# Integer seed of a root in one step, a moved offset, and two first-layer blocks whose high parts come first

## Chip, cores and metric

One Trainium2 chip; the program runs on one core. The metric is the device time of one execution in microseconds (us), taken as the median of several runs; lower is better. Times inside the program are microseconds from the start of the profiled span.

## What is computed

The input `u` has 2048 rows of 512 channels. Two blocks with residuals follow each other:

```
h  = u + S4D(layernorm(u))            # long convolution along the 2048 rows, + D_skip * input
x  = layernorm(h)                     # input of the mixer
t  = gelu(layernorm(x) @ w1)          # 512 -> 512
x1 = x + shift(t) @ w2                # channel quarters shifted by +1, -1, +2, -2 rows
out = h + x1 + gelu(layernorm(x1) @ w3) @ w4     # 512 -> 1792 -> 512
```

Each layernorm needs, for each row, 1/sqrt(variance + 1e-5). Everything is in 32 bits.

## The kernel before

**Two phases.** The convolution phase (`conv_phase`) takes the first 302 us or so. There a planner (`Plan`) with costs and due times sets the order of the instructions. Its last two nodes are `finish(3)` (mean and variance of rows 12 to 15 of each partition, called tiles 12 to 15) and `norm_h` (their roots); they are planned with costs of 0.4 and 2.35. The mixer phase (`mixer_phase`) has its order written out by hand: each engine gets its instructions in the order of the Python calls (class `InOrder`).

**The mixer's first part.** The 2048 rows are 16 tiles of 128 rows in four groups of four; they are worked in the order of groups 3, 0, 1, 2. For a group `q`:

- `finish(q)` computes the statistics and `norms(nc, cst, [q])` the roots, on VectorE (DVE). `norms` writes `ra` (two rows of variances), then `rsqrt_ops` turns them into `rr` with `rb` as scratch, and a last operation makes the offset `rn` = -mean * `rr`. All are tiny: 128 partitions by 8 values. `norms` is called four times, once for each group. `norm2_ops` calls `rsqrt_ops` for the second layernorm, also once for each group, with tiles `qa`, `qb`, `qr`.
- `norm1(q)` normalises the four tiles into `xq`. In group 3, tiles 12, 13 and 15 are normalised on DVE from the mean and `rr` alone; tile 14 is normalised on ScalarE (ACT), which needs the offset `rn`.
- For groups 3 and 0, `turn1(q)` transposes the tiles on TensorE (PE). For groups 1 and 2, `swap` transposes 32x32 blocks on DVE and then moves them with 16 DMAs from the SP and POOL queues. Either way four column chunks come out. Each is split into a high part (rounded, on ACT) and a low part (the rest, on DVE): for group 1 these are `xt10h` to `xt13h` and `xt10l` to `xt13l`.
- `layer1(q, f)` computes output block `f` of the first matrix: 12 matmuls into one PSUM bank. For each of four chunks these are high weight by high input, high weight by low input, low weight by high input. Then `gelu` reads the bank on ACT twice and on DVE once. In the trace, the bank is `l`; the weights live in old buffers of the convolution (`cs0w`, `cs1w`, `sn0w`). In two blocks, (3, 0) and (1, 3), the 12 matmuls are sorted: for (1, 3) all eight with a high input come first, then the four with a low input. The next block, (1, 1), takes them chunk by chunk.
- `layer2(j)` is the shifted second matrix for tile `j`.

After that come 14 steps of the last two matrices, by a scheme with sums of half matrices (`layer3a`, `layer3b`, `layer4a`, `layer4b`); PE banks there are `l3a` to `l3g`, `acc` and `l`.

PSUM banks named `bank` rotate through four buffers, so a block's bank is free once the block four before it has been read.

Of the kernel before, what the change touches and what calls it, by code (L numbers as in the profile page):

```python
# [13 lines left out]
I32 = mybir.dt.int32  # L14
AF = mybir.ActivationFunctionType
ALU = mybir.AluOpType
# [83 lines left out]
class Plan:  # L100
# [15 lines left out]
    def add(self, eng, cost, fn, r=(), w=(), at=None, bank=0, frees=None, dense=1.0, port=None, issue=0):  # L116
        n = len(self.nodes)
        deps = set()
        for k in r:
            if k in self.writer:  # L120
                deps.add(self.writer[k])
            self.readers.setdefault(k, []).append(n)
        for k in w:
            if k in self.writer:
                deps.add(self.writer[k])
            deps.update(self.readers.pop(k, ()))
            self.writer[k] = n
        deps.discard(n)
        if frees is not None:
            deps.add(frees)  # L130
        self.nodes.append(dict(eng=eng, cost=cost, fn=fn, deps=deps, at=at, bank=bank, frees=frees, dense=dense, issue=issue,
                               port=eng == "POOL" if port is None else port))
        return n
# [131 lines left out]
def rsqrt_ops(nc, v, eps, r, a, b):  # L265

    ops = [] if v is None else [lambda: nc.vector.tensor_scalar(a, v, eps, None, ALU.add)]  # L270
    ops += [
        lambda: nc.vector.tensor_scalar(b.bitcast(I32), a.bitcast(I32), 1, None, ALU.logical_shift_right),
        lambda: nc.vector.tensor_scalar(
            r.bitcast(I32), b.bitcast(I32), -1.0, float(0x5E824D95), ALU.mult, ALU.add),
        lambda: nc.vector.tensor_tensor(b, r, r, ALU.mult),
        lambda: nc.vector.scalar_tensor_tensor(b, b, 64.0 / 9.0, a, ALU.mult, ALU.mult),
        lambda: nc.vector.scalar_tensor_tensor(b, b, -10.0 / 3.0, b, ALU.add, ALU.mult),
        lambda: nc.vector.scalar_tensor_tensor(r, b, 5.0, r, ALU.add, ALU.mult),
        lambda: nc.vector.tensor_tensor(b, r, r, ALU.mult),
        lambda: nc.vector.scalar_tensor_tensor(b, b, -0.5, a, ALU.mult, ALU.mult),  # L280
        lambda: nc.vector.scalar_tensor_tensor(r, b, 1.5, r, ALU.add, ALU.mult),
    ]
    return ops
# [9 lines left out]
def norms(nc, cst, qs):  # L293

    ra, rb, rr, nb = cst["norm"]
    mv, t = cst["mv"], slice(qs[0] * 4, qs[-1] * 4 + 4)
    return [
        lambda: nc.vector.tensor_scalar(ra[:, 0, t], mv[:, t, 1], EPS, None, ALU.add),
        lambda: nc.vector.tensor_scalar(ra[:, 1, t], mv[:, t, 1], 1.0 + EPS, EPS * EPS, ALU.mult, ALU.add),
        *rsqrt_ops(nc, None, None, rr[:, :, t], ra[:, :, t], rb[:, :, t]),  # L300
        lambda: nc.vector.scalar_tensor_tensor(
            nb[:, :, t], mv[:, t, 0].unsqueeze(1).to_broadcast([128, 2, len(qs) * 4]), -1.0, rr[:, :, t], ALU.mult, ALU.mult),
    ]
# [3 lines left out]
def conv_phase(ctx, tc, cst, tp, h, x, log_A_real, A_imag, C_real, C_imag, log_dt, D_skip, w1, w2, fa, fi, tb, mm_):  # L307
# [4 lines left out]
    nc = InOrder(tc)  # L312
# [8 lines left out]
    add = plan.add  # L321
# [11 lines left out]
    NG, NS = D // CH, len(WID)  # L333
    OFF = [sum(WID[:s]) for s in range(NS + 1)]
    TS = [NOM["t0"]]
# [5 lines left out]
    at = tile("at", [128, 2, 32 * W])  # L341
# [609 lines left out]
    bx, mv = bs[:, :, 0, :], cst["mv"]  # L951
# [129 lines left out]
    for s in range(NS):  # L1081
# [18 lines left out]
        else:  # L1100

            for i, j in enumerate(range(12, 16)):
                add("DVE", 0.48, lambda j=j: v.bn_stats(bs[:, j, 0, :], h[:, j, 0 : OFF[s]]),
                    r=[("h", q, r) for q in range(s) for r in range(WID[q] // 32)] + [("made", s, BS[i])], w=[("bs", j)],
                    at=TS[s] + NOM["st"] + 2 * j)
            last_a_inv(s)

    def finish(q, tiles=range(4)):

        for j in (4 * q + i for i in tiles):  # L1110
            if q < 3:
                v.bn_stats(bs[:, j, 0, :], h[:, j, :])
        for j in (4 * q + i for i in tiles):
            v.bn_aggr(cst["mv"][:, j, :], bs[:, j, 0, :] if q < 3 else bs[:, j].rearrange("p a b -> p (a b)"))

    def norm_h():
        for op in norms(nc, cst, [3]):
            op()


    add("DVE", 0.4, lambda: finish(3), r=["part"], w=["mv"], at=TS[NS])
    add("DVE", 2.35, norm_h, r=["mv"], w=["norm"], at=TS[NS])
    plan.filler = busy
    plan.run()
    return finish
# [3 lines left out]
def mixer_phase(ctx, tc, cst, h, out, finish, w3, w4):  # L1129

    nc = InOrder(tc)
# [13 lines left out]
    def slot(i):  # L1145
        return cst["slab"](i)
# [10 lines left out]
    def bank(name):  # L1157
        return ps.tile([128, 512], F32, tag="bank", name=name)
# [18 lines left out]
    PROD = ((0, 0), (0, 1), (1, 0))  # L1177
    W1, W2 = cst["w1"], cst["w2"]


    mv = cst["mv"]
    _, _, rr, nb = cst["norm"]
# [28 lines left out]
    H1, XL, XT = {}, {}, {}  # L1211

    def norm1(q):
        XL[q] = []
        for j in range(q * 4, q * 4 + 4):
            t = quarter(XQ[{3: 0, 0: 1, 1: 2, 2: 0}[q]], j % 4)
            if (q < 2 and j % 2) or (q == 3 and j != 14):
                nc.vector.tensor_scalar(t, h[:, j, :], mv[:, j, 0:1], r12[:, j : j + 1], ALU.subtract, ALU.mult)
            else:
                nc.scalar.activation(t, h[:, j, :], AF.Identity, scale=r12[:, j : j + 1], bias=off12[:, j : j + 1])  # L1220
            XL[q].append(t)
# [21 lines left out]
        return hi, lo  # L1243

    def layer1(q, f, later=False):
        b = bank(f"l1_{q}_{f}")
        n = 0
        seq = [(c, wi, xi) for c in range(4) for wi, xi in PROD]
        if (q, f) in ((3, 0), (1, 3)):

            seq.sort(key=lambda k: 2 * k[0] + (3 if q == 3 else 8) * k[2])
        for c, wi, xi in seq:
            nc.tensor.matmul(b, W1[f][wi][:, c * 128 : c * 128 + 128], XT[q][c][xi], start=(n == 0), stop=(n == 11))
            n += 1
        *H1[q, f], low = gelu(b, f"h1_{q}_{f}")
        if later:
            return low
        low()

        tiles = {0: ((15, 0),), 2: ((14, 1), (15, 2)), 1: ((0, 3),), 3: ((0, 4), (1, 5))}[f]  # L1260
        for t, i in tiles:
            if t // 4 != q:
                continue
            for k in range(2):
                src = H1[q, f][k][:, t % 4 * 128 : t % 4 * 128 + 128]
                dst = wrap[k][i // 4][:, i % 4, :]
                if f in (0, 2):
                    nc.gpsimd.tensor_copy(dst[:, 32:128], src[:, 0:96].bitcast(F32))
                    nc.gpsimd.tensor_copy(dst[:, 1:32], src[:, 96:127].bitcast(F32))
                    nc.gpsimd.tensor_copy(dst[:, 0:1], zero)  # L1270
                else:
                    nc.gpsimd.tensor_copy(dst[:, 0:96], src[:, 32:128].bitcast(F32))
                    nc.gpsimd.tensor_copy(dst[:, 96:127], src[:, 1:32].bitcast(F32))
                    nc.gpsimd.tensor_copy(dst[:, 127:128], zero)
# [97 lines left out]
    def raw3(s):  # L1372
        f = s % half
        for i in range(2):
            o = (f + i * half) * 128
            nc.sync.dma_start(raw["ab"[i]].rearrange("p (c f) -> p c f", c=4),
                              w3[:, o : o + 128].rearrange("(c p) f -> p c f", p=128))
# [9 lines left out]
    def load3(s, low=nc.gpsimd, parts=range(3)):  # L1387
        ra, a22, sm_ = raw["a"], raw["b"][:, 256:512], raw["s"]
        if s % 2:
            one, four, last = (slot(11), slot(14)), (slots(4, 2), slots(6, 2)), slot(8)  # L1390
        else:
            one, four, last = (slot(20), W3S[0]), (slots(16, 2), slots(18, 2)), W3S[1]
        for i, (src, (hi, lo)) in enumerate(((ra, one), (sm_, four), (a22, (last[:, 0:256], last[:, 256:512])))):
            if i not in parts:
                continue
            nc.scalar.copy(hi, src)
            low.tensor_tensor(lo, src, hi.bitcast(F32), ALU.subtract)
        at_ = lambda w, i: w[:, i * 256 : i * 256 + 256]
        W3[s] = dict(a11=[at_(w, 0) for w in one], a12=[at_(w, 1) for w in one], a22=[at_(last, i) for i in range(2)],
                     **{f"s{i + 1}": [at_(w, i) for w in four] for i in range(4)})  # L1400
# [14 lines left out]
    def slots(i, n):  # L1415

        k = min(i // 3, 5)
        slot(i)
        o = (i - 3 * k) * 512 + (96 if k == 5 else 0)
        return cst["buffers"][k][:, o : o + n * 512]  # L1420
# [10 lines left out]
    low()  # L1431
    layer2(0), layer2(1)
    norm1(2), sum3()
    third = swap(XQ[0], XQ[1], queues=(nc.sync, nc.gpsimd))
    layer1(1, 3), layer1(1, 1), layer1(1, 0), layer1(1, 2), load3(0), raw3(1)
    layer2(2), layer2(3)
    XT[2] = [parts(v, f"xt2{c}") for c, v in enumerate(third)]
    norm2(0), layer2(4), layer2(5)
# [13 lines left out]
    part = lambda n: [lambda c=c: halve(FT[0, "sums", c][n], 0, n, c) for c in range(2)]  # L1452
# [191 lines left out]
```

## Time and profile before

| | |
|---|---|
| median of 3 runs (lowest, highest) | 690.0 us (689.76, 690.05) |
| profiled execution | 689.87 us |
| its span, first to last instruction | 688.1 us |
| outside the span | 1.77 us |
| mean granted TensorE clock | 0.993 |
| PE busy | 651.2 us (95%) |
| DVE busy | 548.6 us (80%) |
| ACT busy | 408.2 us (59%) |
| POOL busy | 405.0 us (59%) |

The busy share is an average over both phases. What a change in the mixer's first part is worth has to be read there: from the rows in order of time, from what ends each wait of PE, and from the chain of work that ended last. A row of the timeline has its start, its length, the engine, the operation with output and inputs, a count, and in brackets the idle time of the engine before it with what ended it. PEld is the weight load of a matmul, which runs ahead of it; a wait of PE shows there. A row that ends with "x2" merges two instructions.

### The profile page before, as it was taken

The page shows a single profiled execution, that of the slowest core. Times are in us where ns is not written, and L with a number is a line of the kernel's source. Part 1 is how long each engine was busy: PE and PEld are TensorE (multiplying, and loading weights), DVE is VectorE, ACT ScalarE, POOL GpSimd, SP SyncE. Part 2 cuts the span into 40 slices and gives each one's busy share as a digit, 9 for nine tenths or more (in the row PEclk, how much of TensorE's full clock was granted, in tenths as well). Part 3 has the DMA queues.
Part 4 walks back from the last instruction along what each step waited for, and adds up shares of the span by engine and source line. Part 5 has one row for each costly group of instructions (what it writes and reads, how often), then busy time and mean ns, then how long its engine had stood idle before and what let it go on. Part 6 is the DMA issues. An engine that isn't in the chain of part 4 may idle for free.

```text
span 688.1 us, 16792 instructions
## 1 busy us (share of the span) xinstructions
PE 651.2 (95%) x6806; PEld 507.6 (74%) x6806; DVE 548.6 (80%) x960; ACT 408.2 (59%) x706; POOL 405.0 (59%) x422
## 2 busy tenths in 40 slices
PE   5897989999999997989999999999999999999997
PEld 5894756663677684748788888888888888888885
DVE  5998999999898998989978799766879954454554
ACT  7889878967889876245634455544465543444330
POOL 1889589967999999002586209355635555554210
PEclk9998999999999999999999999999999999999999
DMA  8830554011201134010231411133311342211004
GB/s 214 255 149 2 172 169 110 3 48 32 64 3 49 34 96 108 1 60 4 62 92 47 107 31 37 56 93 103 100 44 40 106 130 62 62 46 47 19 13 122
DMA packets 49265, 51.49 MB, mean 75 GB/s; under 512 B 6436, under 2 KB 33060, under 8 KB 49188
## 3 DMA queue, kind: packets, MB, share of 16 engines
q1 hardware_dynamic: 47524, 47.80, 24.2%
q10 hardware_dynamic: 1152, 1.57, 0.9%
q0 software_dynamic: 512, 1.05, 0.6%
q8 instruction: 53, 0.87, 0.5%
q14 instruction: 24, 0.20, 0.1%
HBM read 35.72 MB, written 8.39 MB: 64 GB/s over the span
## 4 chain that ended last, share of the span: by engine, by line
PE 58%; DVE 19%; ACT 12%; issue 4%; POOL 3%; DMA 2%; SPq 1%; DVEq 0%; ACTq 0%; POOLq 0%
PE l L87 19%; PE acc L87 11%; PE bank L87 8%; ACT pt L87 7%; DVE u L87 4%; PE l3e L87 3%; PE l3b L87 3%; PE l3c L87 3%; PE l3a L87 3%; PE l3g L87 3%; PE l3f L87 3%; PE l3d L87 3%; DVE at L87 3%; DVE cs L87 3%; DMA h<-in_A_u_dram 2%
## 5 line engine op out<-in xcount | busy, mean ns | idle before, releaser
L87 ACT ACTIVATE pt<-pt 128x1056 f32<-128x1056 int32 x64 | 69.8, 1091 | 14.4 <-DVE cs L87 6.5
L87 POOL TENSOR_TENSOR pt<-p,s 128x512 int32<-128x512 int32 x64 | 71.8, 1139 | 5.0 <-DVE sn L87 4.1
L87 PE MATMUL bank<-at,tbs 128*64 128x128 f32 (+1 forms) x768 | 63.1, 311 | 3.3 <-DVE u L87 1.6
L87 PEld LDWEIGHTS bank<-at,tbs 128*64 128x64 f32 x768 | 44.6, 134 | 20.5 <-ACT at L87 2.9
L87 PEld LDWEIGHTS bank<-ident 128*128 128x128 f32 x418 | 51.5, 202 | 8.4 <-issue 5.1
L87 PE MATMUL bank<-ident 128*128 128x128 f32 x418 | 55.5, 290 | 0.0
L87 PE MATMUL bank<-u,ms 64*128 64x128 f32 x768 | 50.5, 280 | 3.5 <-DVE at L87 1.3
L87 PEld LDWEIGHTS bank<-u,ms 64*128 64x128 f32 x768 | 45.3, 187 | 8.2 <-issue 1.8
L87 POOL TENSOR_TENSOR cs0w<-raw,cs0w 128x512 fp32r<-128x512 f32 x7 | 9.1, 1300 | 58.9 <-ACT cs0w L87 47.4
L87 DVE TENSOR_TENSOR cs<-pt,amx 128x512 f32<-128x512 f32 x64 | 40.9, 679 | 2.4 <-ACT pt L87 1.3
L87 POOL TENSOR_TENSOR sn1w<-raw,sn1w 128x512 fp32r<-128x512 f32 x7 | 9.6, 1365 | 53.3 <-ACT sn1w L87 40.0
L87 DVE TENSOR_TENSOR h<-h,l 128x512 f32<-128x512 f32 x48 | 32.0, 685 | 10.6 <-PE l L87 10.6
L87 PEld LDWEIGHTS bank<-cs 128*32 128x32 f32 x1024 | 23.9, 111 | 22.0 <-POOL cs L87 6.1
L87 PE MATMUL bank<-cs 128*32 128x64 f32 x1024 | 32.5, 225 | 8.0 <-DVE cs L87 4.6
L87 DVE TENSOR_TENSOR u<-u,l3f 128x512 f32<-128x512 f32 x14 | 9.5, 682 | 36.8 <-PE l3f L87 36.8
L87 ACT ACTIVATE pt<-pt,halfpi 128x1056 f32<-128x1056 f32 x32 | 38.2, 1192 | 0.5
L87 ACT COPY at<-bank 128x512 f32<-128x512 f32 x40 | 24.9, 630 | 22.2 <-PE bank L87 22.1
L87 POOL TENSOR_TENSOR sn<-pt,amp 128x512 f32<-128x512 f32 x30 | 36.8, 1227 | 1.4 <-ACT pt L87 1.0
L87 DVE STREAM_TRANSPOSE at<-bank 128x512 f32<-128x512 f32 (+1 forms) x40 | 35.6, 919 | 2.0 <-PE bank L87 2.0
L87 ACT ACTIVATE u<-u 128x512 f32<-128x512 f32 x56 | 35.4, 632 | 1.8
L87 PE MATMUL bank<-sn 128*32 128x64 f32 x1024 | 31.8, 222 | 2.5 <-DVE sn L87 2.5
L87 POOL TENSOR_TENSOR cs<-pt,amp 128x512 f32<-128x512 f32 x26 | 31.9, 1229 | 3.5 <-ACT at L87 0.9
(1161 smaller groups left out, 2085.3 us busy)
## 6 DMA issues: line engine op xcount, KB each, us to landing
raw<-in_B_w_dram SPq DMA_DIRECT2D x28, 256.0 KB, 2.9
xq<-xq SPq DMA_DIRECT2D x72, 64.0 KB, 2.0
h<-in_A_u_dram SPq DMA_DIRECT2D x32, 128.0 KB, 4.2
h<-in_A_u_dram SPq DMA_DIRECT2D x16, 256.0 KB, 4.0
rawa<-in_B_w_dram SPq DMA_DIRECT2D x14, 256.0 KB, 2.8
rawb<-in_B_w_dram SPq DMA_DIRECT2D x14, 256.0 KB, 2.8
ms<-in_mm_dram SPq DMA_DIRECT2D x4, 768.0 KB, 11.0
out_dram<-h SPq DMA_DIRECT2D x48, 64.0 KB, 1.7
```

What stands on the lines that cost most here:

```text
L87: ins = f(*args, **kw)
```

## The change

1. `rsqrt_ops` made its integer seed in two steps: shift right by one, then multiply by -1 and add a constant. Now it is one step: multiply the integer by -0.5 and add the constant. There is one DVE instruction less in each of eight roots (four of `norms`, four of `norm2_ops`).
2. For group 3, `norm_h` leaves out the offset (the last operation of `norms`); `norm1(3)` issues it right after the first normalised tile, 12. The planned cost of `norm_h` goes from 2.35 to 1.95.
3. Blocks (1, 3) and (1, 1) are issued together (`layer1_two`): the eight matmuls with a high input of the first, the eight of the second, the four with a low input of the first, the four of the second, and then both activations. The second block now goes by highs first as well.

```
 rsqrt_ops:
-        lambda: nc.vector.tensor_scalar(b.bitcast(I32), a.bitcast(I32), 1, None, ALU.logical_shift_right),
         lambda: nc.vector.tensor_scalar(
-            r.bitcast(I32), b.bitcast(I32), -1.0, float(0x5E824D95), ALU.mult, ALU.add),
+            r.bitcast(I32), a.bitcast(I32), -0.5, float(0x5E824D95), ALU.mult, ALU.add),
...
 norm_h:
-        for op in norms(nc, cst, [3]):
+        for op in norms(nc, cst, [3])[:-1]:
             op()
...
-    add("DVE", 2.35, norm_h, r=["mv"], w=["norm"], at=TS[NS])
+    add("DVE", 1.95, norm_h, r=["mv"], w=["norm"], at=TS[NS])
...
 norm1:
                 nc.vector.tensor_scalar(t, h[:, j, :], mv[:, j, 0:1], r12[:, j : j + 1], ALU.subtract, ALU.mult)
+                if j == 12:
+                    norms(nc, cst, [3])[-1]()
...
+    def layer1_two(q, fs):
+
+        seq = [(c, wi, xi) for x in range(2) for c in range(4) for wi, xi in PROD if xi == x]
+        banks = [bank(f"l1_{q}_{f}") for f in fs]
+        for part in (seq[:8], seq[8:]):
+            for f, b in zip(fs, banks):
+                for c, wi, xi in part:
+                    nc.tensor.matmul(b, W1[f][wi][:, c * 128 : c * 128 + 128], XT[q][c][xi],
+                                     start=(c, wi, xi) == seq[0], stop=(c, wi, xi) == seq[-1])
+        for f, b in zip(fs, banks):
+            activate(q, f, b)
...
-    layer1(1, 3), layer1(1, 1), layer1(1, 0), layer1(1, 2), load3(0), raw3(1)
+    layer1_two(1, (3, 1)), layer1(1, 0), layer1(1, 2), load3(0), raw3(1)
```

`activate` is the second half of `layer1`, made a function of its own.

**DVE, end of the convolution and begin of the mixer.** `mvh` holds mean and variance of each tile, `ra`, `rb`, `rr`, `rn` are those of `norms`, `xq` are the normalised tiles. Before:

```order
L87 BN_AGGR mvh<-bs 128x2 x4
L87 TENSOR_SCALAR ra<-mvh 128x4 x2
L87 TENSOR_SCALAR rb<-ra 128x2x4
L87 TENSOR_SCALAR rr<-rb 128x2x4
L87 TENSOR_TENSOR rb<-rr 128x2x4
L87 SCALAR_TENSOR_TENSOR rb<-rb,ra 128x2x4
L87 SCALAR_TENSOR_TENSOR rb<-rb 128x2x4
L87 SCALAR_TENSOR_TENSOR rr<-rb,rr 128x2x4
L87 TENSOR_TENSOR rb<-rr 128x2x4
L87 SCALAR_TENSOR_TENSOR rb<-rb,ra 128x2x4
L87 SCALAR_TENSOR_TENSOR rr<-rb,rr 128x2x4
L87 SCALAR_TENSOR_TENSOR rn<-mvh,rr 128x2x4
```

The three tiles on DVE follow, in one piece. Now the same place reads, from `ra` on:

```order
L87 TENSOR_SCALAR ra<-mvh 128x4 x2
L87 TENSOR_SCALAR rr<-ra 128x2x4
L87 TENSOR_TENSOR rb<-rr 128x2x4
L87 SCALAR_TENSOR_TENSOR rb<-rb,ra 128x2x4
L87 SCALAR_TENSOR_TENSOR rb<-rb 128x2x4
L87 SCALAR_TENSOR_TENSOR rr<-rb,rr 128x2x4
L87 TENSOR_TENSOR rb<-rr 128x2x4
L87 SCALAR_TENSOR_TENSOR rb<-rb,ra 128x2x4
L87 SCALAR_TENSOR_TENSOR rr<-rb,rr 128x2x4
L87 TENSOR_SCALAR xq_3946<-h,mvh,rr 128x512
L87 SCALAR_TENSOR_TENSOR rn<-mvh,rr 128x2x4
L87 TENSOR_SCALAR xq_3946<-h,mvh,rr 128x512 x2
```

The first `rb` is gone, and `rn` stands behind tile 12, ahead of tiles 13 and 15. Everything that DVE does ahead of this place keeps its order, and so does everything on PE, ACT, POOL and SP up to here.

**PE, first two blocks of group 1.** `l_1_3` and `l_1_1` are the banks of blocks (1, 3) and (1, 1); the first input is the chunk, `h` or `l` at its end for high or low. Before:

```order
L87 MATMUL l_1_3_4401<-xt10h,sn0w 128x512 x2
L87 MATMUL l_1_3_4401<-xt11h,sn0w 128x512 x2
L87 MATMUL l_1_3_4401<-xt12h,sn0w 128x512 x2
L87 MATMUL l_1_3_4401<-xt13h,sn0w 128x512 x2
L87 MATMUL l_1_3_4401<-xt10l,sn0w 128x512
L87 MATMUL l_1_3_4401<-xt11l,sn0w 128x512
L87 MATMUL l_1_3_4401<-xt12l,sn0w 128x512
L87 MATMUL l_1_3_4401<-xt13l,sn0w 128x512
L87 MATMUL l_1_1_4420<-xt10h,cs0w 128x512
L87 MATMUL l_1_1_4420<-xt10l,cs0w 128x512
```

Now, from the last chunk of the first block's highs on:

```order
L87 MATMUL l_1_3_4397<-xt13h,sn0w 128x512 x2
L87 MATMUL l_1_1_4398<-xt10h,cs0w 128x512
L87 MATMUL l_1_1_4398<-xt10h,cs1w 128x512
L87 MATMUL l_1_1_4398<-xt11h,cs0w 128x512
L87 MATMUL l_1_1_4398<-xt11h,cs1w 128x512
L87 MATMUL l_1_1_4398<-xt12h,cs0w 128x512
L87 MATMUL l_1_1_4398<-xt12h,cs1w 128x512
L87 MATMUL l_1_1_4398<-xt13h,cs0w 128x512
L87 MATMUL l_1_1_4398<-xt13h,cs1w 128x512
L87 MATMUL l_1_3_4397<-xt10l,sn0w 128x512
L87 MATMUL l_1_3_4397<-xt11l,sn0w 128x512
L87 MATMUL l_1_3_4397<-xt12l,sn0w 128x512
```

The first low input is now the 17th of 24 matmuls and no longer the ninth. The instructions behind these two blocks keep their order on PE, ACT, POOL and SP.

**DVE, second layernorm of group 0.** `mv` holds the statistics of its four tiles, `qa`, `qb`, `qr` are the root's tiles. It is the fifth of the eight roots; before:

```order
L87 TENSOR_SCALAR qa<-mv_0_4351 128x4
L87 TENSOR_SCALAR qb<-qa 128x4
L87 TENSOR_SCALAR qr<-qb 128x4
L87 TENSOR_TENSOR qb<-qr 128x4
L87 SCALAR_TENSOR_TENSOR qb<-qb,qa 128x4
L87 SCALAR_TENSOR_TENSOR qb<-qb 128x4
```

Now:

```order
L87 TENSOR_SCALAR qa<-mv_0_4347 128x4
L87 TENSOR_SCALAR qr<-qa 128x4
L87 TENSOR_TENSOR qb<-qr 128x4
L87 SCALAR_TENSOR_TENSOR qb<-qb,qa 128x4
L87 SCALAR_TENSOR_TENSOR qb<-qb 128x4
```

One operation fewer stands ahead of the ACT operations that use this root; on DVE nothing but such rows and the moved `rn` differs between the two programs.

More of the change, by code (lines that the diff above doesn't have):

```diff
@@ L1245, in layer1, with activate @@
     def layer1(q, f, later=False):
+        seq = [(c, wi, xi) for c in range(4) for wi, xi in PROD]
+        if (q, f) == (3, 0):
+            seq.sort(key=lambda k: 2 * k[0] + 3 * k[2])
         b = bank(f"l1_{q}_{f}")
[L1247 to L1252, printed above, removed]
-            nc.tensor.matmul(b, W1[f][wi][:, c * 128 : c * 128 + 128], XT[q][c][xi], start=(n == 0), stop=(n == 11))
-            n += 1
+        for n, (c, wi, xi) in enumerate(seq):
+            nc.tensor.matmul(b, W1[f][wi][:, c * 128 : c * 128 + 128], XT[q][c][xi], start=(n == 0), stop=(n == 11))
+        return activate(q, f, b, later)
+    def layer1_two(q, fs):
[8 more added lines that the diff above has]
+            activate(q, f, b)
+    def activate(q, f, b, later=False):
         *H1[q, f], low = gelu(b, f"h1_{q}_{f}")
```

## The prediction

> **What bounds the kernel now.** I read the page first, then the chain that ended last in order of time, then the waits of PE's weight loads.
>
> ```profile
> span 688.1 us, 16792 instructions
> PE 651.2 (95%) x6806; PEld 507.6 (74%) x6806; DVE 548.6 (80%) x960; ACT 408.2 (59%) x706; POOL 405.0 (59%) x422
> ```
>
> PE is busy for 95% of the span; that average says nothing on a single stage. The chain does (start, length, what):
>
> ```profile
> 302.75 0.18 DVE rb L87
> ...
> 302.96 0.19 DVE rr L87
> ...
> 304.38 0.18 DVE rr L87
> ...
> 304.58 0.06 DVE rn L87
> ...
> 304.69 0.05 DVEq L87
> ...
> 304.79 0.05 DVEq L87
> ...
> 304.89 1.46 DVE xq L87 x3
> ...
> 339.22 0.61 DVE xt13l L87
> ...
> 339.88 57.68 PE l L87 x253
> ```
>
> From here to 339.83 it runs mostly on DVE (DVEq is its queue's wait instructions); from 339.88 it stays on PE to the end but for the last store. The weight loads show where PE waits between:
>
> ```profile
> 310.19 0.19 PEld L87 LDWEIGHTS l<-xt33l,cs0w 128*128 128x128 f32 x1 [0.24 <-DVE xt33l L87]
> ...
> 336.60 0.41 PEld L87 LDWEIGHTS l<-xt10h,sn0w 128*128 128x128 f32 x2
> ...
> 338.12 0.30 PEld L87 LDWEIGHTS l<-xt13h,sn0w 128*128 128x128 f32 x2 [0.17 <-ACT xt13h L87]
> ...
> 339.87 0.19 PEld L87 LDWEIGHTS l<-xt13l,sn0w 128*128 128x128 f32 x1 [0.42 <-DVE xt13l L87]
> ...
> 413.36 0.19 PEld L87 LDWEIGHTS acc<-cs0w,h_010l 128*128 128x128 f32 x1 [0.33 <-DVE h_010l L87]
> ...
> 525.56 0.19 PEld L87 LDWEIGHTS l<-sn1w,h_501h 128*128 128x128 f32 x1 [0.18 <-DVE u L87]
> ```
>
> At 310.19 PE takes the last low part of group 3. Then it doesn't wait again until group 1 arrives, with its highs at ACT's pace and its lows at DVE's. Behind 340 it waits twice more, for 0.33 and 0.18 us. So all that is gained ahead of 340 reaches the end, if nothing is late behind it.
>
> **Step 1, group 3's root and offset.** The rows above give the root's pace: `rb` to `rr` is 302.96 - 302.75 = 0.21 us, which the shorter seed saves. Tile 12 starts 0.51 behind the last `rr` (304.38 to 304.89): 0.20 until `rn`, then `rn` and wait instructions. In the changed program tile 12 itself waits for `rr`, with eight semaphores on its list for seven, so I subtract the 0.20 for `rn` and add one wait instruction of 0.10 (the two DVEq rows stand 0.10 apart): 0.41, or 0.10 less (bounds: 0.20 less, when the waits run beside `rr`, and nothing). Queued behind this longer wait are only `rn` and tiles 13 and 15, for which PE and ACT wait. Behind tile 12 `rn` costs what it takes where the next operation doesn't need it:
>
> ```profile
> 313.68 0.17 DVE L87 SCALAR_TENSOR_TENSOR rn<-mvh,rr 128x8 f32<-128x8 f32 x1
> 313.76 1.00 DVE L87 TENSOR_SCALAR xq<-h,mvh,rr 128x512 f32<-128x512 f32 x2
> ```
>
> 0.08 from start to start (at most the 0.20 of a dependent pair). So tile 15 is ready 0.21 + 0.10 - 0.08 = 0.23 earlier (bounds 0.01 and 0.33). [...]
>
> What else could hold PE there:
>
> ```profile
> 304.64 0.59 ACT L87 COPY h<-bank 128x512 f32<-128x512 f32 x1 [0.53 <-PE bank L87]
> 305.12 0.82 ACT L87 ACTIVATE xq<-h,rn,rr 128x512 f32<-128x512 f32 x1
> ...
> 305.54 1.94 PE L87 MATMUL xt<-ident,xq 128*128 128x128 f32 x16 [0.98 <-ACT h L87]
> ...
> 305.81 0.54 DVE L87 TENSOR_SCALAR xq<-h,mvh,rr 128x512 f32<-128x512 f32 x1
> ```
>
> PE's transposes start 0.1 behind tile 12's end (304.89 + 0.54), but they may not start before ACT's last copy of the convolution has freed the banks (305.23), so at most 0.25 can be gained. On tile 14 ACT now waits for the later `rn`: that ends at about 304.17 (the last `rr`, 0.21 earlier) + 0.41 + 0.46 (a tile's pace, 304.89 to 305.81 for two) + 0.17 = 305.21, ACT starts at 305.25, not 305.12, and ends at 306.07. Tile 15 ends at 306.35 - 0.23 = 306.12, so tile 14 is hidden by 0.05. **I take 0.23** for xt33l and for PE from 310.19 on.
>
> **Step 2, the way to group 1.** PE has no wait in
>
> ```profile
> 320.00:336.80 16.80, 16.80 (x75) 13.90 (x75) 15.94 (x49) 7.68 (x15) 7.88 (x31) 1.00 0.25 62
> ```
>
> (length, then PE busy, at granted clock 1.00), so it asks for xt10h 0.23 earlier, at 336.37. DVE gains more: 0.23, then 0.21 in each of the next roots, 0.44 at 313.68 and 0.65 behind the third. What follows from there:
>
> ```profile
> 335.89 0.62 ACT L87 CAST xt10h<-xq 128x512 fp32r<-128x512 f32 x1 [3.22 <-DVE rr L87]
> ...
> 334.00 0.27 DVE L87 TENSOR_SCALAR rb<-ra 128x8 int32<-128x8 int32 x1
> 334.31 0.46 DVE L87 TENSOR_SCALAR rr<-rb 128x8 int32<-128x8 int32 x1
> ...
> 337.32 0.69 DVE L87 TENSOR_TENSOR xt10l<-xq,xt10h 128x512 fp32r<-128x512 f32 x1 [0.62 <-ACT xt11h L87]
> ```
>
> DVE's transposes, the 16 DMAs that SP and POOL issue behind them (both queues are idle ahead of these), and ACT's casts come 0.65 earlier; the profile names DVE as releaser of the cast, but what it needs is the landed DMAs. So xt10h ends at 335.86, before PE asks, and the 0.17 wait for xt13h goes. The fourth root saves 0.31 (334.00 to 334.31), or 0.21 if that row is stretched: lows 0.86 to 0.96 earlier. If the DMAs didn't move (bound), the highs would stay ACT's and all but the waits for lows would be lost: a gain of about 0.7, 689.2.
>
> **Step 3, two blocks together.**
>
> ```profile
> 336.82 0.62 PE L87 MATMUL l<-xt10h,sn0w 128*128 128x512 f32 x2
> ...
> 343.00 0.39 PE L87 MATMUL l<-xt10h,cs0w 128*128 128x512 f32 x1
> ...
> 345.72 0.39 PE L87 MATMUL l<-xt10h,cs1w 128*128 128x512 f32 x1
> ...
> 340.81 0.58 ACT L87 ACTIVATE h_3h<-l 128x512 fp32r<-128x512 f32 x1
> ...
> 345.90 0.78 DVE L87 TENSOR_TENSOR h_3l<-gh,h_3h 128x512 fp32r<-128x512 f32 x1
> ```
>
> The two blocks take 343.00 - 336.82 = 6.18; the next one, without waits, 345.72 - 343.00 = 2.72 or 0.227 a matmul, so two take 5.44. **0.74** is what waiting costs. Now 16 highs come first: from 336.59 they last to 340.22, and xt13l, the last low to be taken, is there from 339.83 - 0.9 = 338.9 on. No wait is left. With the shorter seeds alone, in the old order, xt13l would be loaded at 336.37 + 11 x 0.227 = 338.87, about when it is ready, so the steps overlap: the new order alone is worth about 0.7 and adds about 0.1 to the roots. What it delays, the activation of (1, 3), from 340.81 to about 341.3 on ACT, is covered: DVE comes to it only at 345.90. The second bank, taken 1.5 earlier, was emptied by the activation of block (0, 2), the last on ACT before its idle time from 332.67 to 335.89.
>
> **Sum.** 0.23 + 0.74 = 0.97 at 343. The profiled execution took 689.87 us (span 688.1 and 1.77 around it): 689.87 - 0.97 = **688.9**. It lies 0.13 under the median of 690.0, within the spread of the runs.
>
> **What is late next.** I looked for the tightest place behind 343:
>
> ```profile
> 355.49 2.53 POOL L87 TENSOR_TENSOR h<-h,xq 128x512 f32<-128x512 f32 x2
> 356.73 1.84 DVE L87 TENSOR_TENSOR xt20l<-xq,xt20h 128x512 fp32r<-128x512 f32 x1 [0.96 <-ACT xt23h L87]
> ...
> 360.50 0.17 DVE L87 TENSOR_SCALAR qb<-qa 128x4 int32<-128x4 int32 x1
> 360.70 0.17 DVE L87 TENSOR_SCALAR qr<-qb 128x4 int32<-128x4 int32 x1
> ...
> 370.42 1.21 POOL L87 TENSOR_TENSOR raws<-rawb 128x256 f32<-128x256 f32 x1
> 370.95 1.23 DVE L87 TENSOR_TENSOR h_3l<-gh,h_3h 128x512 fp32r<-128x512 f32 x1
> ...
> 372.24 0.19 PEld L87 LDWEIGHTS l<-amp0w,h_3l 128*128 128x128 f32 x1
> ```
>
> h_3l of group 2 ends at 372.18 and is loaded at 372.24: no slack at all. PE comes 0.97 earlier, so DVE must too. Its chain to there goes through POOL's sums behind group 1 (0.9 earlier, with the lows) and the fifth root, where the removed row is 0.20: 1.1 earlier, enough by 0.1. Without that root the gain would end at 0.9. The other three second roots are hidden by PE, whose two later waits stand far from them; I cost them at nothing.
>
> **Rivals.** (a) *The gain is cut at group 2.* DVE's operations are stretched when POOL works beside them (xt20l 1.84 beside POOL's two sums, xt13l 0.61 without). If this train comes only 0.65 earlier (step 2 without the fourth and fifth root), PE waits 0.32 for h_3l: 689.2. For it speaks the missing slack; against it, that POOL's train has the same releasers and moves along.
> (b) *Slower: POOL holds DVE at 370.* h_3l sits beside a POOL operation of 1.21 and lasts 1.23. If DVE loses two more such turns ahead of h_3l, it is 2.4 late; 0.1 is slack, so PE waits 2.3: 688.9 + 2.3 = 691.2. It decides from a delay of 1.1 on. Against it: both trains keep their order. The Trainium skill, SBUF — State Buffer, section "SBUF: two separate sides", describes the port pair of the two engines as an exclusive lock, held for the whole instruction; the stretched rows agree.
> (c) *More than forecast.* Step 1 gives 0.25 and both later waits go, because DVE gains more than PE behind the second roots: 689.87 - 0.25 - 0.74 - 0.33 - 0.18 = 688.4. Against it: DVE works there on PE's banks and moves with PE.
> (d) *The change doesn't do what it says*: a lower planned cost could move the convolution. The order of instructions excludes it; no chance.
>
> **How the numbers follow.** Forecast (gain 0.7 to 1.2): 0.66. (a): 0.20. (b): 0.05, of it 0.04 above the bound. (c): 0.09. A measurement of this kernel can tell about 0.2%, 1.4 us, from no change, so the forecast itself is "same": faster 0.09, same 0.87, slower 0.04. The range, 688.4 to 689.6, reaches to (c), takes in (a) and the bounds of step 1 and of the DMAs (689.1 and 689.2), and leaves out little but (b).
>
> **What would show it.** Right: tile 15 ends about 0.2 earlier, the load of xt33l at 309.96; 24 matmuls of 5.44; no bracket on a load of group 1; h_3l's load at 371.27, without a wait. Wrong: tile 12 not earlier than 304.68; brackets on xt1 loads; a new wait between 343 and 413.

## The result, and the profile after

| | before | changed |
|---|---|---|
| median, us (lowest to highest, runs) | 689.75 (688.72 to 690.87, 22) | 688.57 (687.55 to 689.9, 22) |
| ratio, 95% interval | | 0.9986 (0.9979 to 0.9992) |
| profiled execution, its span | 689.87, 688.1 | 688.42, 686.6 |

The ratio is a gain of 0.97 us (0.0014 of 689.75), between 0.55 and 1.45; the medians differ by 1.18. The forecast was 0.97. The sum held. The first of its two terms did not, and a part that was costed at nothing made up for it.

The page of the changed kernel: the chain that ended last runs on PE for 61% of the span and on DVE for 14% (this line read PE 58% and DVE 19% before).

```profile
span 686.6 us, 16785 instructions
...
PE 61%; DVE 14%; ACT 12%; DMA 4%; POOL 4%; issue 3%; SPq 2%; DVEq 0%; ACTq 0%; POOLq 0%
```

In order of time, changed kernel, end of the convolution (start, length, engine, operation; in brackets the idle time ahead and its releaser):

```profile
300.82 0.89 DVE L87 BATCH_NORM_STATS2 bs<-bank 128x6 f32<-128x128 f32 x4 [1.46 <-PE bank L87]
...
303.77 0.17 DVE L87 SCALAR_TENSOR_TENSOR rr<-rb,rr 128x8 f32<-128x8 f32 x1
304.22 0.58 ACT L87 COPY h<-bank 128x512 f32<-128x512 f32 x1 [0.53 <-PE bank L87]
...
304.38 0.55 DVE L87 TENSOR_SCALAR xq<-h,mvh,rr 128x512 f32<-128x512 f32 x1 [0.44 <-PE bank L87]
...
304.84 0.16 DVE L87 SCALAR_TENSOR_TENSOR rn<-mvh,rr 128x8 f32<-128x8 f32 x1
304.92 1.00 DVE L87 TENSOR_SCALAR xq<-h,mvh,rr 128x512 f32<-128x512 f32 x2
...
305.16 0.81 ACT L87 ACTIVATE xq<-h,rn,rr 128x512 f32<-128x512 f32 x1 [0.35 <-DVE rn L87]
...
306.56 0.58 ACT L87 CAST xt30h<-xt 128x512 fp32r<-128x512 f32 x1 [0.58 <-PE xt L87]
...
309.75 0.19 PEld L87 LDWEIGHTS l<-xt33l,cs0w 128*128 128x128 f32 x1
```

The first row, the statistics of the last four tiles, started at 301.22 before. Nothing ahead of it is in another order, so these 0.40 us are no work of the change (the first experiment shows that they come and go). I call its start M and count everything from it. The last `rr` is then at M + 2.95 for M + 3.16 before: the 0.21 of the removed row. But tile 12 starts 0.61 behind it, not 0.41, and the bracket on it names PE. The load of xt33l, for which the 0.23 of step 1 was taken, starts at M + 8.93 for 8.97 before: 0.04 earlier.

The two blocks and what follows:

```profile
336.37 0.61 PE L87 MATMUL l<-xt10h,sn0w 128*128 128x512 f32 x2
...
338.05 0.69 DVE L87 TENSOR_TENSOR xt13l<-xq,xt13h 128x512 fp32r<-128x512 f32 x1
...
340.46 0.19 PEld L87 LDWEIGHTS l<-xt13l,sn0w 128*128 128x128 f32 x1
...
341.81 0.39 PE L87 MATMUL l<-xt10h,cs0w 128*128 128x512 f32 x1
...
369.65 1.23 DVE L87 TENSOR_TENSOR h_3l<-gh,h_3h 128x512 fp32r<-128x512 f32 x1
...
371.06 0.19 PEld L87 LDWEIGHTS l<-amp0w,h_3l 128*128 128x128 f32 x1
...
412.03 0.19 PEld L87 LDWEIGHTS acc<-cs0w,h_010l 128*128 128x128 f32 x1 [0.22 <-DVE h_010l L87]
...
524.13 0.19 PEld L87 LDWEIGHTS l<-sn1w,h_501h 128*128 128x128 f32 x1 [0.19 <-DVE u L87]
```

The 24 matmuls take 341.81 - 336.37 = 5.44, no load of group 1 has a bracket, and h_3l ends 0.18 ahead of its load. One wait of before is gone in this list, and the prediction had not seen it:

```profile
445.26 0.19 PEld L87 LDWEIGHTS l<-sn1w,h_101h 128*128 128x128 f32 x1 [0.29 <-DVE u L87]
```

### The profile page after: what moved, and what is told of

It is laid out like the page before. It is cut to its first block, busy times and chain, and to the rows that moved or that the text cites. A ratio compares the mean times of both kernels' runs of the same rounds, so it can differ in the third digit from the quotient of the medians.

```text
span 686.6 us, 16785 instructions
## 1 busy us (share of the span) xinstructions
PE 649.7 (95%) x6806; PEld 506.7 (74%) x6806; DVE 547.7 (80%) x952; ACT 408.0 (59%) x706; POOL 404.7 (59%) x422
## 4 chain that ended last, share of the span: by engine, by line
PE 61%; DVE 14%; ACT 12%; DMA 4%; POOL 4%; issue 3%; SPq 2%; DVEq 0%; ACTq 0%; POOLq 0%
PE l L87 24%; PE acc L87 11%; ACT pt L87 7%; PE bank L87 6%; DVE u L87 4%; DVE at L87 3%; PE l3a L87 3%; PE l3b L87 3%; PE l3g L87 3%; PE l3d L87 3%; PE l3f L87 3%; PE l3e L87 3%; PE l3c L87 3%; DVE cs L87 2%; DMA h<-in_A_u_dram 2%
```

## The experiments

All profiles side by side, each value from the rows named, as a difference of starts. "Tile 12" is behind the start of ACT's last copy of the convolution (304.22 above); "blocks" is from xt10h's first matmul to the first of the third block of group 1; "last matmul" is the start of the last row of PE. The last three columns count from M.

| kernel | M | tile 12 | blocks | third block | last matmul | end of span |
|---|---|---|---|---|---|---|
| before | 301.22 | 0.25 | 6.18 | 41.78 | 382.06 | 386.88 |
| before, again | 301.38 | 0.24 | 6.15 | 41.70 | 381.96 | 386.82 |
| offset only | 300.23 | 0.20 | 6.06 | 41.69 | 381.96 | 386.87 |
| order only | 300.23 | 0.27 | 5.79 | 41.45 | 382.05 | 386.87 |
| seed in the second four roots | 300.85 | 0.25 | 6.07 | 41.71 | 381.63 | 386.55 |
| seed in the first four roots | 300.20 | 0.16 | 5.55 | 41.02 | 381.41 | 386.30 |
| seed only | 301.46 | 0.15 | 5.51 | 40.98 | 381.00 | 385.84 |
| seed only, again | 300.93 | 0.16 | 5.53 | 41.01 | 381.07 | 385.87 |
| seed and order | 300.34 | 0.16 | 5.45 | 40.94 | 380.96 | 385.76 |
| changed | 300.82 | 0.16 | 5.44 | 40.99 | 381.01 | 385.78 |
| changed, again | 301.18 | 0.16 | 5.44 | 40.96 | 380.94 | 385.72 |
| changed, short root | 301.33 | 0.15 | 5.44 | 41.00 | 380.93 | 385.77 |
| long seed | 300.25 | 0.45 | 6.28 | 42.49 | 383.43 | 388.25 |

The last row of PE, of before and of the changed kernel:

```profile
683.28 0.39 PE L87 MATMUL l<-amp0w,h_1311h 128*128 128x512 f32 x1
```

```profile
681.83 0.39 PE L87 MATMUL l<-amp0w,h_1311h 128*128 128x512 f32 x1
```

Equal kernels agree within 0.08 at the third block and within 0.10 at the last matmul, while M varies by 1.26. So the profiles tell two or three tenths apart that the times can't. The end of the span, in which the expectations are written, is printed to 0.1 us only, so a value in the last column can be off by 0.05; where a tenth matters, I go by the last matmul. On average it is at 381.99 in the three kernels with the old seeds and the old order, at 381.04 in the two with the seed only, and at 380.98 in the two of the changed kernel: 0.96 of the 1.02 us is the seed's (differences of the unrounded means).

Before again, offset only, short root and long seed were executed once each (690.01, 688.87, 688.84 and 690.32 us); for these four I use the marks alone.

**Before, again** (no edit).

> The kernel before, unchanged, profiled once more. In the first pair of profiles the first statistics row of the last four tiles started at 301.22 us before and at 300.82 after, though nothing ahead of it is in another order. Theory (it varies by itself): the row starts anywhere from 300.8 to 301.6 here, and the PE rows behind it keep their distances (xt10h's first matmul 35.60 behind it, the third block of group 1 41.78 behind it). Rival (the change moved the convolution): the row starts at 301.22 within 0.05 again.

M came at 301.38, and over all profiles anywhere from 300.20 to 301.46 with the same order of instructions. The convolution varies by itself; the 0.40 isn't the change's. xt10h's first matmul stood at 35.55 and the third block at 41.70, 0.05 and 0.08 from the first profile.

**Seed only.**

```
-        lambda: nc.vector.tensor_scalar(b.bitcast(I32), a.bitcast(I32), 1, None, ALU.logical_shift_right),
         lambda: nc.vector.tensor_scalar(
-            r.bitcast(I32), b.bitcast(I32), -1.0, float(0x5E824D95), ALU.mult, ALU.add),
+            r.bitcast(I32), a.bitcast(I32), -0.5, float(0x5E824D95), ALU.mult, ALU.add),
```

> The one-step seed alone; the offset and the order of the blocks as before. Theory S (the two edits overlap, as predicted): the lows of group 1 come about 0.7 earlier by the roots alone, the two blocks take 5.44 to 5.65 us instead of 6.18, and the time falls by 0.6 to 0.8 us. Rival O (the order is what removes the waits): the blocks still take about 6.0, and the time falls by 0.2 to 0.3. On the root of group 3: theory W (tile 12 pays for its own wait instructions) has tile 12 at 0.51 behind the last rr, so 0.21 earlier against ACT's last copy of the convolution (0.04 behind that copy's start for 0.25 before); theory E (tile 12 waits for the last matmul of the convolution, as that copy does) has it not under 0.16 behind the copy's start.

687.68 against 688.95 us, ratio 0.9983 (0.9974 to 0.9991), 1.17 us. The blocks take 5.51 with the old order; one wait for a low is left:

```profile
304.88 0.59 ACT L87 COPY h<-bank 128x512 f32<-128x512 f32 x1 [0.54 <-PE bank L87]
...
305.03 1.46 DVE L87 TENSOR_SCALAR xq<-h,mvh,rr 128x512 f32<-128x512 f32 x3 [0.25 <-PE bank L87]
...
339.36 0.19 PEld L87 LDWEIGHTS l<-xt13l,sn0w 128*128 128x128 f32 x1 [0.16 <-DVE xt13l L87]
```

Rival O fell. Theory S held in its mechanism and was too low in size: the gain is 1.17 by the ratio and 0.96 at the last matmul, where S said 0.6 to 0.8. Tile 12 starts 0.15 behind the copy, where theory W said 0.04 and theory E 0.16 or more: theory E held.

**Order only.** The seeds and the offset stay as before; the blocks are those of the change.

```
-    layer1(1, 3), layer1(1, 1), layer1(1, 0), layer1(1, 2), load3(0), raw3(1)
+    layer1_two(1, (3, 1)), layer1(1, 0), layer1(1, 2), load3(0), raw3(1)
```

> The two blocks issued together, highs first; seeds and offset as before. The 24 matmuls should take 5.44 us and at most the 0.17 wait for xt13h on top (5.61): 0.57 to 0.74 less than before. Theory Z (no slack behind): DVE's train to h_3l of group 2 is not earlier, since the lows of group 1 are not; h_3l ends 70.96 behind the start of the statistics rows as before, and PE waits 0.4 to 0.6 us for it, so the time falls by 0.0 to 0.2 us only. Rival K (DVE follows PE): h_3l comes earlier with PE, no wait there, the time falls by 0.55 to 0.75 us.

689.36 against 688.95, ratio 1.0004 (0.9995 to 1.0014): nothing, and the last matmul at 382.05 isn't earlier than before either. The trace shows where the gain stayed:

```profile
335.89 0.30 PEld L87 LDWEIGHTS l<-xt10h,sn0w 128*128 128x128 f32 x2 [0.36 <-ACT xt10h L87]
...
336.41 0.30 PEld L87 LDWEIGHTS l<-xt11h,sn0w 128*128 128x128 f32 x2 [0.23 <-ACT xt11h L87]
...
336.94 0.30 PEld L87 LDWEIGHTS l<-xt12h,sn0w 128*128 128x128 f32 x2 [0.22 <-ACT xt12h L87]
...
337.45 0.30 PEld L87 LDWEIGHTS l<-xt13h,sn0w 128*128 128x128 f32 x2 [0.22 <-ACT xt13h L87]
...
369.92 1.22 DVE L87 TENSOR_TENSOR h_3l<-gh,h_3h 128x512 fp32r<-128x512 f32 x1
...
371.19 0.19 PEld L87 LDWEIGHTS l<-amp0w,h_3l 128*128 128x128 f32 x1 [0.31 <-DVE h_3l L87]
```

With the old seeds the highs come at ACT's pace, 0.52 from load to load, and PE waits for each of the four. So the blocks take 5.79, more than the 5.61 at most that was expected under either theory. What is won (41.45 for 41.7) is given back at h_3l, which ends at M + 70.91 for 70.96 before. Theory Z held: 0.31 of wait there (0.4 to 0.6 expected, since less was won), no gain at the end.

**Seed and order, the offset as before.** The diff is that of the change without its three lines on the offset and the planned cost.

> Seeds and order of blocks as in the changed kernel, the offset of group 3 where it was before the change, ahead of tile 12. Theory W (wait instructions behind rr set tile 12): tile 12 starts 0.51 behind the last rr instead of 0.61, tile 15 ends 0.18 earlier than in the changed kernel, 4.92 behind the start of the statistics rows, and so does PE from group 3's last low part on. Theory E (the last matmul of the convolution sets tile 12): tile 12 starts about 0.16 behind ACT's last copy as in the changed kernel, whatever the root does; only the 0.08 that the offset cost between tiles 12 and 13 is won, tile 15 ends at 5.02. The time is then that of the changed kernel or 0.1 us less under either.

687.84 against 688.95, ratio 0.9984 (0.9975 to 0.9993). Tile 12 is 0.16 behind the copy again, xt30h's cast starts at M + 5.60 for 5.74 in the changed kernel, and the last matmul is at 380.96 (381.01 and 380.94 in the changed kernel). Tile 15 ends at M + 5.04. Theory E held: a root that is over earlier doesn't bring tile 12 forward.

**Short root.** The changed kernel without the last three operations of group 3's root.

```
-        for op in norms(nc, cst, [3])[:-1]:
+        for op in norms(nc, cst, [3])[:-4]:
```

> The changed kernel with the last three operations of group 3's first root left out (the second Newton step; group 3 is normalised with a less exact root). The root is 0.60 shorter. Theory E: tile 12 still starts 0.16 behind the start of ACT's last copy, with the idle time of DVE ahead of it grown from 0.44 to about 1.04; xt30h's cast stays at 5.74, the end at 385.7 to 385.85. Theory W: tile 12 starts 0.60 earlier, ahead of that copy's start by 0.44.

```profile
303.69 0.17 DVE L87 SCALAR_TENSOR_TENSOR rr<-rb,rr 128x8 f32<-128x8 f32 x1
...
304.73 0.59 ACT L87 COPY h<-bank 128x512 f32<-128x512 f32 x1 [0.54 <-PE bank L87]
...
304.88 0.55 DVE L87 TENSOR_SCALAR xq<-h,mvh,rr 128x512 f32<-128x512 f32 x1 [1.03 <-PE bank L87]
```

The root ends 0.6 earlier against M, and tile 12 doesn't move against the copy; DVE is idle for 1.03 instead of 0.44. Theory W is refuted by 0.6 us. The copy and tile 12 wait for the same PE work, and the program says so: tile 12's list of semaphores,

```
L87 TENSOR_SCALAR xq_3946<-h,mvh,rr 128x512 [waits DMAHW0_49,DMAHW1_49,DVE_49,DMAHW2_49,PE_49,DMAHW7_49,Activation_49,Pool_49]
```

has a count of PE that the very last matmul of the convolution brings. Its result goes to rows that tile 12 doesn't read; `xq` lies in memory that the convolution gives up, which is the likely reason for the wait (argued, not tried). ACT's last copy waits for the same count.

**Offset only.** The three lines on the offset alone.

> The offset of group 3 behind tile 12, seeds and blocks as before. Theory E (tile 12 waits for the last matmul of the convolution, at which ACT's last copy starts): tile 12 starts 0.16 to 0.26 behind the start of that copy (before 0.24 to 0.27), the 0.08 of the offset then comes on top for tiles 13 and 15, and xt30h's cast starts 5.70 to 5.77 behind the statistics rows (before 5.68). Theory W (tile 12's own wait instructions, 0.61 behind rr): tile 12 0.35 behind the copy's start, the cast at 5.85 to 5.90. Under both the edit alone gains nothing, and the end lies 386.8 to 387.0 behind the mark.

Tile 12 at 0.20, the cast at M + 5.78 (0.01 beyond theory E's range, 0.07 under W's; before 5.69), the end at 386.87. Tile 12 starts 0.45 behind the last `rr` here, with the last matmul and the root over at nearly the same time; so the 0.41 of the prediction was near for the wait on the root, and what it left out was the matmul. The cast is 0.09 later, and that is hidden: with the old roots PE waits for ACT and DVE at group 1 anyway.

**Seed in the first four roots, seed in the second four.** `v` is given only where `rsqrt_ops` is called for the second layernorm.

```
     ops += [
         lambda: nc.vector.tensor_scalar(b.bitcast(I32), a.bitcast(I32), 1, None, ALU.logical_shift_right),
         lambda: nc.vector.tensor_scalar(
             r.bitcast(I32), b.bitcast(I32), -1.0, float(0x5E824D95), ALU.mult, ALU.add),
+    ] if v is not None else [
+        lambda: nc.vector.tensor_scalar(
+            r.bitcast(I32), a.bitcast(I32), -0.5, float(0x5E824D95), ALU.mult, ALU.add),
+    ]
+    ops += [
```

This is the first; the second has `if v is None`.

> The one-step seed in the first four roots alone; the four roots of the second layernorm keep the two steps, offset and order of the blocks as before. Marks count from the start of the statistics rows of the last tiles. Theory P (the gain has two parts, ahead of and behind the first layer): the third block of group 1 starts at 40.95 to 41.05 as with all seeds (before 41.70 to 41.78); at h_3l of group 2 PE waits 0.0 to 0.1; the waits of 0.33 near 413 and of 0.29 near 445 are back; the end of the span lies 386.0 to 386.15 behind the mark (before 386.82 to 386.88, all seeds 385.76 to 385.84), so the gain is 0.7 to 0.8 for 1.05. Rival Q (as the prediction costs it, the second roots are worth nothing but the fifth's 0.2): the wait for h_3l is the only difference from all seeds, the end at 385.8 to 385.95.

> The one-step seed in the four roots of the second layernorm alone. Theory P: nothing changes up to the third block of group 1 (41.70 to 41.78 behind the mark), h_3l of group 2 is 0.2 earlier than PE asks, so nothing is won at it; the wait near 413 shrinks by about 0.1 (the sixth root) and the 0.29 near 445 goes (the seventh); the end at 386.5 to 386.65, a gain of 0.2 to 0.35. Rival Q (second roots worth nothing): the end at 386.8 to 386.9, the wait near 445 stays.

Against 688.86 us: 688.24, ratio 0.999 (0.9981 to 0.9999), and 688.49, ratio 0.9993 (0.9984 to 1.0002). The first four roots bring the third block to 41.02 and the end to 386.30; the second four change nothing up to the third block and bring the end to 386.55. The waits tell the two apart; first four, then second four:

```profile
370.46 0.19 PEld L87 LDWEIGHTS l<-amp0w,h_3l 128*128 128x128 f32 x1
...
411.55 0.19 PEld L87 LDWEIGHTS acc<-cs0w,h_010l 128*128 128x128 f32 x1 [0.30 <-DVE h_010l L87]
...
443.48 0.19 PEld L87 LDWEIGHTS l<-sn1w,h_101h 128*128 128x128 f32 x1 [0.29 <-DVE u L87]
```

```profile
524.79 0.19 PEld L87 LDWEIGHTS l<-sn1w,h_501h 128*128 128x128 f32 x1 [0.18 <-DVE u L87]
```

The second list is all that is left behind 343 there: the waits near 413 and 445 are gone. Theory P held in its mechanism, rival Q fell. In size the first four gave 0.58 at the last matmul (381.99 to 381.41) where P said 0.7 to 0.8, and the second four 0.36. The two parts make 0.94, and both together gave 0.96: they add up. The first four roots are 0.70 ahead at the third block and still at a matmul of h_101l at M + 143.62, and 0.58 ahead at M + 167.56; no load in between has a bracket, and what takes the 0.12 is open.

**Changed kernel and seed only, both again** (no edit).

> The changed kernel again, beside the seed alone on the same chip. Theory P (the seed is all of it): the times of the two differ by less than 0.3 us, each 0.8 to 1.3 under the kernel before; against the start of the statistics rows the third block of group 1 starts at 40.95 to 41.05 and the first load of h_1301h at 375.7 to 375.85 in both. Rival R (the order of the two blocks and the moved offset add something): the changed kernel is 0.3 us or more faster than the seed alone.

> The one-step seed alone, a second time. Theory P: as the changed kernel within 0.3 us and within 0.05 at the marks. Rival R: slower than it by 0.3 us or more.

Against 689.45 us: 687.92, ratio 0.9983 (0.9974 to 0.9992), and 688.51, ratio 0.9988 (0.9979 to 0.9996). The medians differ by 0.59, which is what rival R asked for and more than theory P allowed. But the intervals overlap, and in the first pair the seed alone had the lower ratio (0.9983 against 0.9986), so the times can't tell the two apart. The marks are as theory P said: the third block is at 40.96 and 41.01, the first matmul of h_1301h at 375.73 and 375.85. At the last matmul the changed kernel is 0.01 behind the seed alone in the first pair and 0.13 ahead in the second, 0.06 on average, which is inside the 0.10 between equal kernels. Rival R's 0.3 is at no mark; nearly all the gain is the seed's, and whether the order and the offset add anything is not shown.

**Long seed.** A third step, which changes no number, ahead of the two of before.

```
-        lambda: nc.vector.tensor_scalar(b.bitcast(I32), a.bitcast(I32), 1, None, ALU.logical_shift_right),
+        lambda: nc.vector.tensor_scalar(b.bitcast(I32), a.bitcast(I32), 0, None, ALU.logical_shift_right),
+        lambda: nc.vector.tensor_scalar(b.bitcast(I32), b.bitcast(I32), 1, None, ALU.logical_shift_right),
```

> The kernel before with three steps for the seed in place of two (a shift by 0 ahead of the shift by 1): each of eight roots is 0.2 longer. Theory P (each root's length stands on PE's path): the price is as large as the gain was. Tile 12 starts 0.2 later against ACT's last copy (0.45 behind its start), the third block of group 1 at 42.45 to 42.65 (before 41.7), the wait near 445 grows from 0.29 to 0.5, the end lies 387.85 to 388.1 behind the mark (before 386.85). Rival S (the lows had been the only limit, and the rest has slack): up to the third block at most 0.4 is lost, and nothing behind it.

```profile
303.66 0.59 ACT L87 COPY h<-bank 128x512 f32<-128x512 f32 x1 [0.54 <-PE bank L87]
...
304.11 1.46 DVE L87 TENSOR_SCALAR xq<-h,mvh,rr 128x512 f32<-128x512 f32 x3
...
336.46 0.30 PEld L87 LDWEIGHTS l<-xt10h,sn0w 128*128 128x128 f32 x2 [0.72 <-ACT xt10h L87]
...
372.17 0.19 PEld L87 LDWEIGHTS l<-amp0w,h_3l 128*128 128x128 f32 x1 [0.22 <-DVE h_3l L87]
...
410.87 0.19 PEld L87 LDWEIGHTS l3e<-t100h,cs1w 128*128 128x128 f32 x1 [0.30 <-DVE u L87]
...
445.48 0.19 PEld L87 LDWEIGHTS l<-sn1w,h_101h 128*128 128x128 f32 x1 [0.50 <-DVE u L87]
...
466.06 0.19 PEld L87 LDWEIGHTS l<-cs0w,h_201h 128*128 128x128 f32 x1 [0.29 <-DVE u L87]
```

Tile 12 at 0.45, the third block at 42.49, the wait near 445 at 0.50: as theory P said. The end, 388.25, is 0.15 beyond its range, and three waits are new behind the first layer (372.17, 410.87 and 466.06). One DVE operation of 0.2 in each of eight roots costs 1.4 us here (last matmul 381.99 to 383.43) where taking one away gained 1.0. In this direction tile 12 does follow the root: behind the last matmul's release the root is the later of the two.

## Why the prediction came out as it did

**The root's row, 0.21: right.** The last `rr` moved from M + 3.16 to M + 2.95.

**Tile 12 at 0.41 behind `rr`: wrong, and this is the step that failed.** "In the changed program tile 12 itself waits for `rr`", so its wait was built from wait instructions alone. It waits for the convolution's last matmul too, which before was over at about the time when `rn` ran; DVE was busy there, so no bracket showed it. The row that could have shown it was quoted: ACT's last copy, at 304.64, waits for that matmul, and tile 12 came only 0.25 behind it. With a floor of 0.15 (short root) the shorter root could win 0.1, of which the moved `rn` takes 0.08 back. I had set that copy as a bound for PE's transposes alone. In all, tile 12 started 0.11 earlier (M + 3.67 to 3.56) and tile 15 ended 0.03 earlier (M + 5.13 to 5.10), where 0.23 was forecast. The prediction's own sign of being wrong, tile 12 not earlier than 304.68, came true: 304.38 with M 0.40 earlier is 304.78 on the clock of before.

**`rn` for 0.08 behind tile 12: right** (304.84 to 304.92, and 0.07 in three other profiles). The Trainium skill, VectorE: DVE Perf Modes, section "The DRAIN you can't avoid", says that the next operation doesn't start until the pipe has emptied, and then that a next operation that is not held back starts earlier; the trace agrees with the second, for tile 13 starts 0.08 behind the start of an `rn` that lasts 0.16.

**Tile 14 hidden by 0.05: wrong.** ACT starts it at 305.16 and ends it at 305.97, behind tile 15 (305.92). The cast of xt30h therefore starts at M + 5.74, for 5.60 with `rn` ahead of tile 12. The moved offset costs 0.14 there, with the new seed; at the last matmul nothing of it is seen (381.01 and 380.94 against 380.96).

**Step 1 as a whole, 0.23:** xt10h's first matmul moved from a mean of M + 35.59 (35.60, 35.55 and, with the offset only, 35.63) to 35.55 and 35.52, so about 0.06, and the load of xt33l from a mean of M + 8.96 to 8.92, so 0.04: inside the bounds of 0.01 and 0.33 but at their low end.

**Step 2: right for the lows but for what it took over from step 1.** DVE's `rn` of the second root is 0.25 earlier (M + 12.46 to 12.21; 0.44 had been forecast), and xt10l behind the fourth 0.69 (36.10 to 35.41; at least 0.86): about 0.22 in each of these roots, with most of step 1 missing. For the highs 0.65 had been forecast, and ACT's cast of xt10h came 0.35 earlier in the first two profiles (M + 34.67 to 34.32). In the program it waits for all 16 DMAs, and it varies by itself: from M + 34.67 to 34.99 in the four profiles with the old first roots and offset. No load of group 1 waits in the changed kernel.

**Step 3, 5.44 for two blocks: right to the hundredth, but credited to the wrong edit.** (The 0.74 that it saves is that of the first profile; against the mean of the three with the old order, 6.13, it is 0.69.) "The new order alone is worth about 0.7" failed: alone it won 0.27 at the third block, because the highs then come at ACT's pace, and nothing at the end, because h_3l had no slack. The bound "if the DMAs didn't move" stood next to that sentence and held the mechanism; I didn't carry it over to the order alone. "Adds about 0.1 to the roots" was right for the blocks (5.51 and 5.53 with the seed only, 5.44 with both).

**What is late next: half right.** h_3l without slack is confirmed by the order alone (0.31 of wait). In the changed kernel it ends 0.18 early. PE asks for it 0.78 earlier than before (M + 71.02 to 70.24), not 0.97. The fifth root wasn't needed for that lead: without it (first four roots) h_3l ends at 370.39, its load is at 370.46 and has no bracket. Rivals (a) and (b) didn't happen; h_3l still lasts 1.23.

**"The other three second roots are hidden": wrong.** The second four roots win 0.36 alone, and with their seed the wait near 445 goes. The prediction counted two waits behind 340 and missed the third, at 445.26; all hang on DVE, which comes to them from its roots. Rival (c) had the idea (DVE gains more there than PE) and the wrong rows: the wait near 525 stays at 0.19, the one near 413 shrinks to 0.22 or goes, the one near 445 goes.

**The sum, 0.97, came out by two errors against each other.** Counted from M, the changed kernel gains 1.02 at the last matmul (381.99 to 380.98, rounded means), of it 0.75 up to the third block (41.72 to 40.98), where 0.97 had been forecast, and 0.27 behind it, where nothing had been. That the ratio gives 0.97 as well is luck: its interval is 0.9 us wide.

## What to carry to other kernels

An instruction that starts right behind a busy engine shows no wait, though it may have one: before shortening what runs ahead of it, look up its whole list of semaphores and find another instruction that waits for the same event, since its start is the floor. When two edits attack the same wait, price each of them alone against the trace: here a 0.2 us operation taken out of a chain that is passed eight times did nearly everything, and the new order alone nothing. Look up how many digits a mark is printed with before reading a tenth from it. And go through every bracket on the bounding engine's loads to the very end of the span; small ones far behind a change belong to it where the same chain runs ahead of them.

## What was not expected of the hardware

The convolution, with its instructions in one and the same order, ended anywhere within 1.26 us in thirteen profiles (M from 300.20 to 301.46), while equal kernels repeated the start of the last matmul, counted from M, to 0.10. The granted clock between 30 and 60 us doesn't sort them: it was 0.94 in the profile with M at 301.38 and in one with 300.23. What does is open. Not all behind M holds as still: the cast of xt10h, behind 16 DMAs, started anywhere from M + 34.67 to 34.99 in the four profiles with the old first roots and offset, whose instructions have the same order up to it. For changes of under 1 us behind M, counting from M resolves about 0.1, where the runs of one kernel are spread over 2 us.

Small dependent DVE operations (128x8 or 128x4, 0.17 each) cost 0.20 from start to start, and their removal and addition moved the program by five and by seven times one of them, 1.0 and 1.4 us, for eight roots.
